# Delta-rule attention and two MoE layers on one core: order of the start, a joint product in step 1, PSUM rings by step, and reordered lists and tokens

## The chip, the cores and the metric

The kernel runs on one core of one Trainium2 chip as one program. The metric is the device time of an execution in microseconds (us). Before the change the median of three executions is 841.74 us (840.85 to 842.69).

## The reference

Inputs: q, k, v of shape (4 batches, 8 heads, 768 positions, 48), beta (4, 8, 768); float64 weights for the first MoE layer, float32 for the second. Three layers follow each other.

```python
# 1 attention, per batch and head, 768 positions in sequence
k_n = k / (norm(k) + 1e-6)
y[t] = q[t] @ state
state = state + beta[t] * outer(k_n[t], v[t] - k_n[t] @ state)
# 2 first MoE, x is y laid out as 3072 tokens x 384
x = ((x @ w1) * (x @ w2)) @ w3 @ w_out          # 384 -> 1024 -> 1024 -> 384
# 3 second MoE, 8 experts, each token goes to one
logits = x @ w_gate + modality_bias[modality_id]
e = argmax(logits); gate = softmax(logits)[e]
out = gate * (relu(x @ e_w1[e]) @ e_w2[e])      # 384 -> 1024 -> 384
```

## The kernel before, in words

**Engines and order.** Each engine runs its instructions in the order in which the program issues them: every call goes through `Engine` (L86), which chains an instruction to the one before it on its engine. All of them therefore carry line 86 in the profile, and groups are told apart by tile names. What sets the order is the code itself: the loop over `f` in `moe1`, the calls of `slot(s, f)`, the generators that are advanced one step at a time, and the table `do` in `startup`.

**Numbers.** A float32 product is made of three passes on a high part (rounded to float32r) and a low part (the rest): high by high, low by high, high by low. So nearly every tensor is split: ScalarE copies the high part, VectorE or GpSimd subtracts it to get the low one.

**The start** (`startup`, L561 on) walks a list `todo` of 36 tiles: 8 of w_out, 16 of w3 and 12 of w1 and w2, all float64 in memory. `tick(n)` issues for tile n+1 the magnitude `mag` and the low word (two ScalarE instructions, `scalar`), for tile n two VectorE operations that join them to a float32 (`vector`), then by `flush` what has come due of earlier tiles, then the next load (`issue`) and the products (`use`). `use` folds w3 and w_out into one matrix `w34` (PSUM tile `pw`) and queues the split of a tile (`w34h`, `w34l`, and for w1 and w2 `w`) as one function that makes the high part on ScalarE and the low part on VectorE. w_out, in float32, lies in tiles `wos`; five of its eight rows lie in the space of `X[1]`, so `X[1]` can be cleared or filled only when the last folded tile's products with them are done. Between the ticks `do` inserts the first steps of the attention: gram matrices, the 31-step triangular inverse on VectorE (`tmp`, `Tt`), step 0.

**Attention** takes the positions in 12 steps of 64; a unit is two steps. In step s `chain_k` multiplies the keys with the state (`X[..., 0:48]`), for s > 1 jointly with the queries that lie beside it (`X[..., 48:112]`) in four PSUM tiles `pkq`, takes R = v - that, and `mask_parts` masks the query part on VectorE: the first two tiles at once, the others when `slot` comes to f = 1. `chain_u` gives `pu`, `chain_y` the output `py`, `chain_s` the new state. Step 1 is done otherwise: keys alone (`pk`), and later the queries (`pq`) in `masked`, masked on VectorE. The loads of the queries of steps 1 and 2 are issued in step 1, f = 0. PSUM tiles come from two rings of two buffers, `ps` and `pc`: of a step's four `pkq` the first two lie in `ps` and the others in `pc`, where `pu` lies too.

**First MoE** (`moe1`): twelve blocks of 256 tokens, eight f each; nine products each for w1 and w2 into `pAB`, their product `a` split into `ch` and `cl`, and two f later the products with `w34` into `px`. `slot(i + 1, f)` puts a piece of attention ahead of each f. The end of a block routes its tokens; `place` ranks them one block later (`pr`; then `hot`, one-hot rows and columns; then `pl`, which is added to `list`).

**Second MoE** (`moe2`): 14 slots of up to 256 tokens of one expert. `back(i)` runs eight f of nine products each into `ph`, its split `hh` and `hl`, and two f later six products into `spy`. `ahead` advances the splitting of later weights (`w1h`, `w1l`, `w2h`, `w2l`) and, at f = 1, 2, 3, the tokens of the next slot: a transpose `spt` of gathered rows `xg`, split into `sxh` and `sxl`. During slots 0 to 2 the generator `late` runs one step per f: the last block's `place`, then `listed`, then the tables of the later slots.

## Time and profile before

| | |
|---|---|
| median of 3 executions | 841.74 us |
| the profiled execution | 841.03 us |
| its span, first to last instruction | 839.3 us |
| TensorE busy | 786.3 us, 94% of the span |
| VectorE busy | 618.8 us, 74% |
| ScalarE busy | 408.9 us, 49% |
| GpSimd busy | 165.6 us, 20% |
| mean granted TensorE clock | 0.968 of full speed |

The profile describes one execution, so sums are made against its 841.03 us; 1.7 us of that lie outside the span. The median of the runs is 0.7 us above it. An engine's idle time counts only where another engine, in the end TensorE, waits for it; the busy share is an average over stages with different limits.

### The profile page before, as it was taken

The numbers are of one execution on the slowest core, as the hardware profiler recorded it, in microseconds if no ns is written. First come the engines' busy times: TensorE is split into PE (matmuls) and PEld (weight loads), VectorE is DVE, ScalarE is ACT, GpSimd is POOL, SyncE is SP. The second block draws the span as 40 slices with busy tenths as digits, with TensorE's granted clock in tenths as the row PEclk, the third lists the DMA queues.
The fourth block names the chain that finished last, engine by engine and source line by source line (L and its number), as shares of the span: only waits on it lengthen the run. The fifth ranks groups of instructions, "written<-read, shape, count | busy, mean of one in ns | idle before, by whom it ended". The sixth has DMA issues, their size and how long they took to land.

```text
span 839.3 us, 23624 instructions
## 1 busy us (share of the span) xinstructions
PE 786.3 (94%) x9583; PEld 730.6 (87%) x9583; DVE 618.8 (74%) x1573; ACT 408.9 (49%) x863; POOL 165.6 (20%) x172
## 2 busy tenths in 40 slices
PE   5797789999999999999999999999899999999994
PEld 5664468999999899989998999999799999999983
DVE  5998889769777976897689864567886778677651
ACT  6467673562546154524543353334455655655541
POOL 3021121100000001000100000013254654645420
PEclk8598899999999999999999999999999999999997
DMA  9952563314121421133021401047457678677610
GB/s 310 280 176 87 151 161 102 75 35 120 54 51 38 116 65 40 40 115 82 23 65 39 102 13 31 27 131 222 151 177 246 215 249 258 227 225 238 220 56 6
DMA packets 71812, 105.34 MB, mean 126 GB/s; under 512 B 33988, under 2 KB 53332, under 8 KB 71696
## 3 DMA queue, kind: packets, MB, share of 16 engines
q1 hardware_dynamic: 64464, 88.35, 34.7%
q0 software_dynamic: 4064, 11.06, 3.9%
q10 hardware_dynamic: 3168, 4.34, 1.5%
q8 instruction: 77, 1.26, 0.6%
q14 instruction: 39, 0.32, 0.1%
HBM read 89.15 MB, written 10.63 MB: 119 GB/s over the span
## 4 chain that ended last, share of the span: by engine, by line
PE 46%; DVE 26%; issue 11%; ACT 7%; POOL 4%; DMA 3%; SPq 1%; POOLq 0%; DVEq 0%; ACTq 0%
PE pAB L86 13%; PE px L86 9%; PE ph L86 7%; PE spy L86 4%; DVE tmp L86 4%; DVE Tt L86 4%; DVE X L86 3%; DVE TT L86 2%; PE pw L86 2%; DVE Ab L86 2%; ACT TT L86 2%; PE pkq L86 2%; PE pg L86 2%; DVE a L86 2%; PE py L86 2%
## 5 line engine op out<-in xcount | busy, mean ns | idle before, releaser
L86 PE MATMUL pAB<-x,w 128*128 128x256 f32 x1728 | 228.8, 286 | 0.0
L86 PEld LDWEIGHTS pAB<-x,w 128*128 128x128 f32 x1728 | 213.9, 191 | 4.4
L86 ACT CAST ch<-a 128x256 fp32r<-128x256 f32 x96 | 39.0, 406 | 116.4 <-DVE a L86 116.4
L86 ACT COPY a<-pAB 128x256 f32<-128x256 f32 x96 | 35.6, 371 | 116.9 <-PE pAB L86 104.3
L86 DVE TENSOR_TENSOR a<-a,pAB 128x256 f32<-128x256 f32 x96 | 40.0, 416 | 65.6 <-ACT a L86 65.3
L86 PE MATMUL ph<-sxh,w1h 128*128 128x256 f32 x288 | 82.5, 286 | 0.5 <-DVE hl L86 0.5
L86 ACT ACTIVATE hh<-ph 128x256 fp32r<-128x256 f32 x96 | 37.0, 385 | 91.7 <-PE ph L86 91.5
L86 PE MATMUL ph<-sxl,w1h 128*128 128x256 f32 x288 | 81.2, 282 | 0.0
L86 PE MATMUL ph<-sxh,w1l 128*128 128x256 f32 x288 | 81.2, 282 | 0.0
L86 DVE SCALAR_TENSOR_TENSOR hl<-ph,hh 128x256 fp32r<-128x256 f32 x96 | 40.3, 420 | 41.0 <-ACT hh L86 40.5
L86 DVE TENSOR_TENSOR Tt<-tmp,Tt 128x31 f32<-128x31 f32 (+15 forms) x186 | 64.3, 346 | 6.4
L86 DVE TENSOR_TENSOR w2l<-r,w2h 128x768 fp32r<-128x768 f32 x56 | 59.5, 1074 | 12.2 <-ACT w2h L86 11.9
L86 DVE TENSOR_TENSOR tmp<-Ab,Tt 128x31 f32<-128x31 f32 (+15 forms) x186 | 65.4, 352 | 3.0
L86 PE MATMUL px<-w34h,ch 128*128 128x392 f32 x192 | 65.6, 342 | 0.0
L86 PE MATMUL px<-w34h,cl 128*128 128x392 f32 x192 | 65.3, 340 | 0.0
L86 PE MATMUL px<-w34l,ch 128*128 128x392 f32 x192 | 65.2, 339 | 0.0
L86 POOL TENSOR_TENSOR w1l<-r,w1h 128x512 fp32r<-128x512 f32 x39 | 51.0, 1327 | 49.9 <-ACT w1h L86 49.6
L86 DVE TENSOR_TENSOR cl<-a,ch 128x256 fp32r<-128x256 f32 x96 | 43.0, 447 | 20.1 <-ACT ch L86 19.3
L86 PEld LDWEIGHTS ph<-sxh,w1h 128*128 128x128 f32 x288 | 54.7, 190 | 1.3 <-DVE hl L86 1.1
L86 PEld LDWEIGHTS ph<-sxh,w1l 128*128 128x128 f32 x288 | 54.8, 190 | 0.0
L86 PEld LDWEIGHTS ph<-sxl,w1h 128*128 128x128 f32 x288 | 54.6, 190 | 0.0
L86 ACT CAST w1h<-r 128x512 fp32r<-128x512 f32 x84 | 49.5, 615 | 2.9 <-DMA r<-in_e_w_dram 2.5
(269 smaller groups left out, 1677.7 us busy)
## 6 DMA issues: line engine op xcount, KB each, us to landing
r<-in_e_w_dram SPq DMA_DIRECT2D x42, 512.0 KB, 4.7
r<-in_e_w_dram SPq DMA_DIRECT2D x56, 384.0 KB, 3.9
raw<-in_w_dram SPq DMA_DIRECT2D x28, 512.0 KB, 4.6
kT<-in_kt_dram SPq DMA_DIRECT2D x12, 512.0 KB, 4.5
X<-in_q_dram SPq DMA_DIRECT2D x24, 256.0 KB, 4.8
vt<-in_v_dram SPq DMA_DIRECT2D x12, 384.0 KB, 4.7
kb<-in_kb_dram SPq DMA_DIRECT2D x12, 384.0 KB, 4.7
x2d<-xr ACTq DMA_DIRECT2D x22, 192.5 KB, 2.8
```

Of the source, the lines that this page charges most:

```text
L86: x = f(*a, **kw)
```

## The change

- **Start.** The split of a tile is queued as two entries, one in `high` (ScalarE) and one in `low` (VectorE). `tick` issues the due high parts ahead of the next tile's magnitude, and the low parts where both were before. `flush`, which the last ticks call first, now issues other work, then high parts, then low parts.
- **Step 1** takes the joint form that the later steps have. Its masks are made by a ScalarE copy and a GpSimd select for each half tile (eight of each) in place of four VectorE products. The queries of steps 1 and 2 are loaded at the last folded tile of the start.
- **Rings by step.** In odd steps the first two `pkq` lie in `pc` and the others in `ps`; in even steps as before.
- **Second MoE.** In slots 0 to 2 `late` issues `pl` one f later (f = 4). In slot 0 the next slot's tokens are issued ahead of the weights of the same f; in slot 2 they come at f = 3, 4, 5.

```diff
         if f == 0:
             self.chain_k(s)
-            if s == 1:
-                self.queries(1)
-                self.queries(2)
         elif f == 1:
             if c == 0:
                 list(self.merge1(u))
                 next(self.work, None)
                 if more:
                     self.work = self.inverse(u + 1)
-            if s > 1:
-                list(self.masks)
+            list(self.masks)
         elif f == 2:
             list(self.chain_u(s) if c else self.merge2(u))
-            if s == 1:
-                list(self.masked(s))
             if s + 1 < NS:
                 self.values(s + 1)
         elif f == 3:
...
+                nc.scalar.copy(W[o:o + C, h, a:a + HP], pq[o:o + C])
+                nc.gpsimd.affine_select(out=W[o:o + C, h, a:a + HP], in_=W[o:o + C, h, a:a + HP], pattern=[[0, HP], [1, C]], compare_op=ALU.is_gt, fill=0.0, base=0, channel_multiplier=-1)
...
-        if s > 1:
...
-                pool, tag = ((self.ps, "ps"), (pc, "pc"))[q // 2]
...
-            self.R = R
-            self.masks = self.mask_parts(s, todo)
-            next(self.masks)
-            return
-        for a in self.halves:
-            pk = pc.tile([P, HP, D], F32, tag="pc", name="pk")
-            for n, m, h in self.tiles(a):
-                o, w = (1 - h) * C, h * C
-                nc.tensor.matmul(pk[o:o + C, m], kT[w:w + C, n0 + n], X[w:w + C, h, n, 0:D], start=True, stop=True)
-            nc.vector.tensor_tensor(out=R[:, a:a + HP], in0=vt[:, a:a + HP], in1=pk, op=ALU.subtract)
+        todo = []
+        for q, a in enumerate(range(0, NP, NQ)):
+            pool, tag = ((self.ps, "ps"), (pc, "pc"))[(q // 2 + s) % 2]
+            pk = pool.tile([P, NQ, D + C], F32, tag=tag, name="pkq")
+            for m in range(NQ):
+                for h in range(2):
+                    o, w = (1 - h) * C, h * C
+                    nc.tensor.matmul(pk[o:o + C, m], kT[w:w + C, n0 + a + m], X[w:w + C, h, a + m], start=True, stop=True)
+            todo.append((a, pk))
+        for a, pk in todo:
+            nc.vector.tensor_tensor(out=R[:, a:a + NQ], in0=vt[:, a:a + NQ], in1=pk[:, :, 0:D], op=ALU.subtract)
         self.R = R
+        self.masks = self.mask_parts(s, todo)
+        next(self.masks)
 
     def mask_parts(self, s, todo):
 
@@ -483,6 +464,10 @@
         for q, (a, pk) in enumerate(todo):
             for h in range(2):
                 o = (1 - h) * C
+                if s == 1:
+                    self.nc.scalar.copy(W[o:o + C, h, a:a + NQ], pk[o:o + C, :, D:])
+                    self.nc.gpsimd.affine_select(out=W[o:o + C, h, a:a + NQ], in_=W[o:o + C, h, a:a + NQ], pattern=[[0, NQ], [1, C]], compare_op=ALU.is_gt, fill=0.0, base=0, channel_multiplier=-1)
+                    continue
                 self.nc.vector.tensor_tensor(out=W[o:o + C, h, a:a + NQ], in0=pk[o:o + C, :, D:], in1=mb[o:o + C], op=ALU.mult)
             if q == 1:
...
+        raw, out, mag, after, high, low = {}, {}, {}, [], [], []
...
-            due = n + 1 if kind == "w" else min(n + 2, FC) if kind == "o" else n + (2 if n < FC + AHEAD else 4)
+            when = min(n + 2, FC) if kind == "o" else n + (2 if n < FC + AHEAD else 4)
...
-                def f():
-                    nc.scalar.copy(self.w34[0][:, r], pw)
-                    nc.vector.tensor_tensor(out=self.w34[1][:, r], in0=pw, in1=self.w34[0][:, r].bitcast(F32), op=ALU.subtract)
+                high.append((when, lambda: nc.scalar.copy(self.w34[0][:, r], pw)))
+                low.append((when, lambda: nc.vector.tensor_tensor(out=self.w34[1][:, r], in0=pw, in1=self.w34[0][:, r].bitcast(F32), op=ALU.subtract)))
+                return
             else:
                 m, g, kk = x
                 t = wp.tile([P, 2, DCH], F32R, tag=f"w{m}{g}{kk}", name=f"w{m + 1}")
                 hi, lo = self.w12[m][0][g][kk], self.w12[m][1][g][kk] = t[:, 0], t[:, 1]
 
-                def f():
-                    nc.scalar.copy(hi, out[n])
-                    nc.vector.tensor_tensor(out=lo, in0=out[n], in1=hi.bitcast(F32), op=ALU.subtract)
-            after.append((due, f))
+                high.append((n + 1, lambda: nc.scalar.copy(hi, out[n])))
+                low.append((n + 1, lambda: nc.vector.tensor_tensor(out=lo, in0=out[n], in1=hi.bitcast(F32), op=ALU.subtract)))
+                return
+            after.append((when, f))
+
+        def due(n, lists):
+            for x in lists:
+                now = [y for y in x if y[0] <= n]
+                x[:] = [y for y in x if y[0] > n]
+                yield from (f for _, f in now)
 
         def flush(n):
-            now = [f for due, f in after if due <= n]
-            after[:] = [x for x in after if x[0] > n]
-            for f in now:
+            for f in due(n, (after, high)):
+                f()
+            for f in due(n, (low,)):
                 f()
 
         def tick(n):
             self.n = n
             if n >= NSTART - 2:
                 flush(n)
+            for f in due(n, (high,)):
+                f()
             scalar(n + 1)
             vector(n)
-            flush(n)
+            for f in due(n, (low, after)):
+                f()
             issue()
             use(n)
...
         folded = todo.index(("3", K3 - 1))
-        do.setdefault(folded, []).append(self.clear)
+        do.setdefault(folded, []).extend([self.clear, lambda: self.queries(1), lambda: self.queries(2)])
         do.setdefault(folded + 1, []).append(lambda: split(self.chain_s(0)))
         do.setdefault(NSTART - 1, []).extend([lambda: self.tokens(1), lambda: self.tokens(2)])
...
         def late():
             yield
-            yield from self.place(NT // MT - 1)
+            last = self.place(NT // MT - 1)
+            next(last)
             yield
+            next(last)
+            yield
+            yield
+            list(last)
             yield from self.listed()
             yield
             yield from self.late_slots()
...
             def step(tok, n):
+                if tok and i == 0:
+                    next(toks, None)
                 for _ in range(n):
                     next(work, None)
-                if tok:
+                if tok and i > 0:
                     next(toks, None)
...
-            ahead(f in (1, 2, 3), 1 + (f < 3 if i == 0 else f > 4))
+            ahead(f - 2 * (i == 2) in (1, 2, 3), 1 + (f < 3 if i == 0 else f > 4))
```

What ScalarE is given in the start, one piece of the difference, from the last gram matrices of unit 0 to the root `r` of unit 1 (TT_94 is the space of the converted tiles, TT_93 unit 0's inverse):

```order
 L86 ACTIVATE An<-pg 32x8x32 x2
 L86 COPY TT_93<-TT_93 32x32x32 x2
-L86 ACTIVATE mag<-raw 128x512
-L86 ACTIVATE TT_94<-raw 128x512
 L86 CAST w34h<-pw 128x392
+L86 ACTIVATE mag<-raw 128x512
+L86 ACTIVATE TT_94<-raw 128x512
 L86 ACTIVATE mag<-raw 128x512
 L86 ACTIVATE TT_94<-raw 128x512
 L86 COPY An<-pe 32x16x32 x4
 L86 ACTIVATE r<-ss 128x32
```

The copy of `w34h` moves ahead of one tile's two conversions; the same happens at each later split of the start.

What SyncE's queue is given around the end of the start (X_91 and X_90 hold the queries of steps 1 and 2, raw the float64 tiles, kb the tokens of steps 1 and 2):

```order
 L86 DMA vt<-in_v_dram 128x768
-L86 DMA raw<-in_w_dram 128x512 x13
-L86 DMA kb<-in_kb_dram 128x768 x2
+L86 DMA raw<-in_w_dram 128x512 x12
 L86 DMA X_91<-in_q_dram 64x16x64 x2
 L86 DMA X_90<-in_q_dram 64x16x64 x2
+L86 DMA raw<-in_w_dram 128x512
+L86 DMA kb<-in_kb_dram 128x768 x2
```

The four query loads move ahead of the last float64 tile and of kb; they stood behind both.

TensorE in slot 0 of the second MoE, before, at the end of f = 3:

```order
L86 MATMUL ph<-sxh,w1l 128x256
L86 MATMUL spt<-ident,xg 128x128 x2
L86 LDWEIGHTS hot
L86 MATMUL pl<-hot 128x192
L86 LDWEIGHTS hot
L86 MATMUL pl<-hot 128x192
L86 MATMUL spy<-w2h,hh 128x384
```

And after the change, at the end of f = 4:

```order
L86 MATMUL ph<-sxh,w1h 128x256
L86 MATMUL ph<-sxl,w1h 128x256
L86 MATMUL ph<-sxh,w1l 128x256
L86 LDWEIGHTS hot
L86 MATMUL pl<-hot 128x192
L86 LDWEIGHTS hot
L86 MATMUL pl<-hot 128x192
L86 MATMUL spy<-w2h,hh 128x384
```

The two `pl` now come behind the next f's nine `ph` products; the transposes `spt` stay at the end of f = 3 and are followed there by f = 1's six `spy` products.

## Rows read from the trace of the kernel before

**Rows 1.** The page, part 1: busy time, share, instructions of each engine.

```profile
PE 786.3 (94%) x9583; PEld 730.6 (87%) x9583; DVE 618.8 (74%) x1573; ACT 408.9 (49%) x863; POOL 165.6 (20%) x172
```

**Rows 2.** Busy time by stage: stage, length, PE, PEld, DVE, ACT, POOL, clock, DMA.

```profile
44.00:116.00 72.00, 58.23 (x688) 36.17 (x688) 63.47 (x131) 49.81 (x90) 12.46 (x26) 0.91 0.42 130
116.00:160.00 44.00, 42.00 (x711) 39.21 (x709) 38.28 (x78) 22.38 (x48) 8.01 (x8) 1.00 0.51 135
160.00:570.00 410.00, 404.68 (x6242) 385.32 (x6238) 306.79 (x927) 176.13 (x377) 21.07 (x18) 1.00 0.23 63
```

**Rows 3.** TensorE's waits: waiter, releaser; total us, times, longest us.

```profile
PE pu L86 <- DVE X L86: 4.1, 4, 1.4
...
PE pl L86 <- DVE hot L86: 2.2, 3, 1.8
...
PE spt L86 <- DMA xg<-x2d,id: 1.6, 1, 1.6
...
PE py L86 <- DVE X L86: 1.6, 3, 1.0
...
PE spt L86 <- DVE sxl L86: 1.2, 1, 1.2
...
PE pkq L86 <- DVE list L86: 1.0, 2, 0.6
```

**Rows 4.** VectorE's waits between 44 and 118 us, same columns.

```profile
DVE w34l L86 <- ACT w34h L86: 4.2, 4, 2.7
DVE w L86 <- ACT w L86: 2.4, 2, 1.8
```

**Rows 5.** Timeline of ScalarE: start us, us, engine, line, operation, idle before.

```profile
64.16 2.11 ACT L86 COPY TT<-TT 32x1024 f32<-32x1024 f32 x2 [0.79 <-DVE TT L86]
...
67.62 0.49 ACT L86 CAST w34h<-pw 128x392 fp32r<-128x392 f32 x1
...
87.19 1.94 ACT L86 COPY X<-pu 64x384 f32<-64x384 f32 x4 [5.86 <-PE pu L86]
...
90.20 0.60 ACT L86 CAST w<-TT 128x512 fp32r<-128x512 f32 x1
```

**Rows 6.** Timeline of TensorE from the last folded tile to step 2.

```profile
118.81 2.12 PE L86 MATMUL pk<-X,kT 64*64 64x48 f32 x64 [0.41 <-ACT X L86]
...
127.31 1.97 PE L86 MATMUL pq<-X,kT 64*64 64x64 f32 x60
...
160.44 2.52 PE L86 MATMUL pkq<-X,kT 64*64 64x112 f32 x48 [0.19 <-ACT An L86]
```

**Rows 7.** Timeline of GpSimd: step 0's selects, and the clearing of X.

```profile
53.88 3.33 POOL L86 TENSOR_SCALAR_AFFINE_SELECT X<-X 64x512 f32<-64x512 f32 x4 [45.24 <-ACT X L86]
...
114.98 2.80 POOL L86 MEMSET X<- 32x1536 f32 x2 [19.40 <-PE pw L86]
```

**Rows 8.** Tile X, 118 to 130 us: landing of the queries' four DMAs.

```profile
DMA to landing us min/median/max: 5.7/7.7/8.0
```

**Rows 9.** Tile X, 149 to 160 us: landing of step 3's queries.

```profile
DMA to landing us min/median/max: 5.6/5.6/5.6
```

**Rows 10.** Busy time and granted clock around two falls; columns as in rows 2.

```profile
76.00:78.60 2.60, 0.03 (x1) 0.00 (x0) 2.39 (x9) 2.58 (x5) 0.00 (x0) 1.00 0.24 93
...
78.60:85.40 6.80, 4.54 (x7) 2.52 (x8) 6.39 (x21) 1.26 (x3) 0.00 (x0) 0.50 0.22 78
...
597.40:600.90 3.50, 3.50 (x16) 3.50 (x15) 1.49 (x4) 0.00 (x0) 0.00 (x0) 0.51 0.54 214
```

**Rows 11.** Timeline of VectorE: equal products beside the selects and alone.

```profile
53.98 0.67 DVE L86 TENSOR_TENSOR tmp<-Ab,Tt 128x112 f32<-128x112 f32 x1
...
82.40 0.27 DVE L86 TENSOR_TENSOR tmp<-Ab,Tt 128x112 f32<-128x112 f32 x1
```

**Rows 12.** Timeline of VectorE, slot 0 of the second MoE: hl of f = 2.

```profile
595.54 0.42 DVE L86 SCALAR_TENSOR_TENSOR hl<-ph,hh 128x256 fp32r<-128x256 f32 x1
```

**Rows 13.** Timeline of TensorE, slot 0: pl at the end of f = 3.

```profile
596.75 0.64 PE L86 MATMUL pl<-hot 128*128 128x192 f16 x2 [1.84 <-DVE hot L86]
```

More of the change, by code (lines that the diff above doesn't have):

```diff
@@ L420, in masked @@
         kT, W, n0 = self.st[s // US]["kT"], self.st["W", s], s % US * NP
-        mb = self.mask.unsqueeze(1).to_broadcast([P, HP, C])
         todo = []
@@ L433, in masked @@
                 o = (1 - h) * C
-                if s < 1:
-                    nc.scalar.copy(W[o:o + C, h, a:a + HP], pq[o:o + C])
-                    nc.gpsimd.affine_select(out=W[o:o + C, h, a:a + HP], in_=W[o:o + C, h, a:a + HP], pattern=[[0, HP], [1, C]], compare_op=ALU.is_gt, fill=0.0, base=0, channel_multiplier=-1)
-                    continue
-                nc.vector.tensor_tensor(out=W[o:o + C, h, a:a + HP], in0=pq[o:o + C], in1=mb[o:o + C], op=ALU.mult)
+                nc.scalar.copy(W[o:o + C, h, a:a + HP], pq[o:o + C])
+                nc.gpsimd.affine_select(out=W[o:o + C, h, a:a + HP], in_=W[o:o + C, h, a:a + HP], pattern=[[0, HP], [1, C]], compare_op=ALU.is_gt, fill=0.0, base=0, channel_multiplier=-1)
     halves = range(0, NP, HP)
@@ L454, in chain_k @@
         R = a1.tile([P, NP, D], F32, tag="R", name="R")
-        if s > 1:
-            todo = []
-            for q, a in enumerate(range(0, NP, NQ)):
-                pool, tag = ((self.ps, "ps"), (pc, "pc"))[q // 2]
-                pk = pool.tile([P, NQ, D + C], F32, tag=tag, name="pkq")
-                for m in range(NQ):
-                    for h in range(2):
-                        o, w = (1 - h) * C, h * C
-                        nc.tensor.matmul(pk[o:o + C, m], kT[w:w + C, n0 + a + m], X[w:w + C, h, a + m], start=True, stop=True)
-                todo.append((a, pk))
-            for a, pk in todo:
-                nc.vector.tensor_tensor(out=R[:, a:a + NQ], in0=vt[:, a:a + NQ], in1=pk[:, :, 0:D], op=ALU.subtract)
-            self.R = R
-            self.masks = self.mask_parts(s, todo)
-            next(self.masks)
-            return
-        for a in self.halves:
-            pk = pc.tile([P, HP, D], F32, tag="pc", name="pk")
-            for n, m, h in self.tiles(a):
-                o, w = (1 - h) * C, h * C
-                nc.tensor.matmul(pk[o:o + C, m], kT[w:w + C, n0 + n], X[w:w + C, h, n, 0:D], start=True, stop=True)
-            nc.vector.tensor_tensor(out=R[:, a:a + HP], in0=vt[:, a:a + HP], in1=pk, op=ALU.subtract)
+        todo = []
[9 more added lines that the diff above has]
+            nc.vector.tensor_tensor(out=R[:, a:a + NQ], in0=vt[:, a:a + NQ], in1=pk[:, :, 0:D], op=ALU.subtract)
         self.R = R
+        self.masks = self.mask_parts(s, todo)
+        next(self.masks)
     def mask_parts(self, s, todo):
@@ L586, in startup @@
         free = [f"w{m}1{kk}" for kk in range(KC) for m in range(2)] + ["x0", "x1", "xr"]
-        raw, out, mag, after = {}, {}, {}, []
+        raw, out, mag, after, high, low = {}, {}, {}, [], [], []
         issued = [0]
```

## The prediction

> **What bounds the kernel now.** I read the page's shares first, then busy time by stage, then TensorE's waits, and only then timelines around the places that change. TensorE is busy 94% of the span [rows 1], so the question is what each stage leaves it idle for. From 44 to 116 us it is not the bound: VectorE is busy 63.47 of 72 us, TensorE 58.23 [rows 2]. From 116 us on TensorE is: it idles 2.0 us of 44 up to 160, and 5.3 us of 410 up to 570 [rows 2]. After that its waits are few and have names [rows 3]. So an edit pays in two ways only: it shortens VectorE's chain ahead of 116 us, or it removes one of TensorE's listed waits behind it.
>
> **Start: high parts sooner.** VectorE stands still 4.2 us in four waits for `w34h`, and 2.4 us in two for `w` [rows 4]. The reader is to see why in ScalarE's queue: the copies of the inverse end at 66.27, the cast of `w34h` begins at 67.62, with one tile's two conversions (1.3 us) between [rows 5]; with `pu` likewise, whose copies end at 89.13 while the cast of `w` begins at 90.20 [rows 5]. Now the cast comes first. Three of the four `w34h` waits are 4.2 - 2.7 = 1.5 us together, and go. In the longest, of 2.7 us, the low part starts some 1.3 us sooner, but VectorE's next work is the join of the very tile whose conversions now stand behind the cast (0.5 us): 0.6 us are left. The 1.8 us at `w` shrinks by 1.1 (90.20 - 89.13), and by a little more because `pu` starts sooner too. That is 1.5 + 0.6 + 1.1 = 3.2, with the last effect 3.5 us. The other wait for `w`, 2.4 - 1.8 = 0.6 us, lies behind the last folded tile, where the cast now even stands behind the state's copies; I count nothing for it, since TensorE waits for something else there (next part). Bounds: 2.0 (only the short waits and the conversions' half) and 6.0 (4.2 + 1.8).
>
> **Step 1: the joint form.** It needs fewer products: `pk` 2.12 us and `pq` 1.97 x 64/60 = 2.10 make 4.22; a joint `pkq` of step 2 takes 2.52 x 64/48 = 3.36 [rows 6]. That is -0.9 us on TensorE. The waits of `py` for the masks on VectorE, 1.6 us [rows 3], go: ScalarE and GpSimd make the masks two f ahead of `py`, and the four VectorE products vanish.
>
> But the joint product now needs the queries, and they cannot come early. X[1] holds rows of w_out until the last folded products, and the clearing of X[1], which waits for the same products, starts at 114.98 [rows 7]. The load is issued then at the soonest. Before, `pk` started at 118.81 and needed no queries [rows 6]. The four loads of 118 to 130 us land 5.7 to 8.0 us after issue [rows 8], two alone 5.6 [rows 9]. Both halves of step 1 are needed at once, so the product starts between 120.6 (114.98 + 5.6) and 123.0 (114.98 + 8.0). I take 121.8: the first pair of four, with one float64 tile in flight and a second issue behind the first. Cost: 121.8 - 118.81 = +3.0 us, bounds +1.8 and +4.2, in a place where everything behind it on TensorE, the first MoE included, queues up. On SyncE the last float64 tile and both kb now stand behind four query loads; they are used several us later, so I count nothing; if that cover is gone it shows as waits of ScalarE's last conversions.
>
> TensorE is idle from 118.40 (118.81 - 0.41) until then, 3.4 us. After 2.6 us without work from 76 us on the granted clock was 0.50 for 6.8 us, and it was 0.51 for 3.5 us after the waits of 1.2 and 1.8 us near 592 and 597 [rows 3, 10]. So I expect a fall to 1.2 GHz here too, of the shorter kind: 3.5 us at half clock cost 1.7 us. Bounds 0 and 3.4.
>
> **GpSimd's selects beside VectorE.** Four selects of 64 x 512 take 3.33 us [rows 7], so eight of half the size about as much. Beside them a product of VectorE took 0.67 us where an equal one alone took 0.27 [rows 11]; the one after it reads the same way, 0.8 us in all. VectorE has lost 2.8 us of masks here, so I count nothing; bounds 0 and 3.3, the selects' whole time. The Trainium skill ("SBUF — State Buffer", section "Who interferes with whom") says that a VectorE operation with two SBUF inputs is blocked for the whole of a GpSimd instruction that reads SBUF. By the rule all 3.3 us would be lost on VectorE; the trace shows a quarter, since most of VectorE's work then was not of that kind or not in step with a select.
>
> **Rings by step.** Four times `pu` waits for masks on VectorE, 4.1 us, the longest 1.4 [rows 3]; all four lie in odd steps, because `pu` needs a buffer of `pc` and the late masks (those of f = 1) still read there. In odd steps the early masks now free `pc`, and the late ones hold `ps`. The two waits of `pkq` for `list`, 1.0 us [rows 3], were for the second `ps` buffer and are passed two products later. What is late next is VectorE's product `a`, which frees the PSUM of the f after next; VectorE is idle a quarter of that stage, 410 - 306.79 us [rows 2]. -5.1 us; bounds -5.1 and -1.0.
>
> **Second MoE.** In slot 0 `spt` waits 1.2 us for `sxl`, and `pl` 1.8 us for `hot` [rows 3]. The first shrinks to about 0.5, as the tokens are now split ahead of one weight part. The second goes, but VectorE frees `ph` of f = 2 only at 595.96 (595.54 + 0.42) [rows 12]; TensorE was done with `spt` at 594.91 (596.75 - 1.84) [rows 13], is there 0.6 sooner, at 594.3, and has six `spy` products ahead of that `ph`. So a new wait of less than 1.7 (595.96 - 594.3) takes the old one's place; I take 0.6. So 3.0 - 0.5 - 0.6 = 1.9 us go, and with them the fall of the clock, 3.5 us at half [rows 10], 1.7 us. -3.6; bounds -1.0 and -4.7. In slot 2 `spt` waits 1.6 us for gathered rows [rows 3]; two f later, with some thirty products between, they should have landed. -1.6; bounds 0 and -1.6. `list` itself is issued one f later, but `listed` follows where it did, so tables and gathers don't move.
>
> **The sum**, against the profiled execution's 841.03 us: -3.5 + 3.0 + 1.7 - 0.9 - 1.6 = -1.3 up to step 2; -5.1 for the rings; -3.6 - 1.6 in the second MoE. That is -11.6, so 829.4. The median of the runs lies 0.7 above that execution: 830.1, predicted as 830.
>
> **Rivals.**
> 1. The start brings nothing. Queries land at 8.0 us (+4.2), the clock falls for 6.8 us as at 78.6 (+3.4), the casts give only 2.0: -2.0 + 4.2 + 3.4 - 0.9 - 1.6 = +3.1. With the other terms (-10.3) 833.8. For it: small loads at 8.0 in rows 8; against: less traffic beside them. 0.15.
> 2. The rings move the wait: VectorE, with equal work, makes TensorE wait one product later, only the 1.0 of `list` stays: 829.4 + 4.1 = 833.5. For it: VectorE 306.79 of 410 us busy; against: a quarter of the stage is idle on it. 0.10.
> 3. The start goes well: all 6.0 us of waits gone, landing at 5.6 (+1.8), no fall: 6.0 - 1.8 + 0.9 + 1.6 = 6.7 gained, 841.03 - 6.7 - 10.3 = 824.0. 0.10.
> 4. Selects block VectorE for their whole 3.3 us, and TensorE waits for its products: 832.7. Rows 11 show 0.8 of 3.3, so 0.04. This is the skill's rule named above.
> 5. Slower: the clock falls at the queries' wait and stays low while VectorE, busy 38.28 of 44 us [rows 2], paces TensorE. At half clock from 123 to 155 us that is 32/2 = 16 in place of 1.7, with 1.2 for the later landing: 829.4 + 14.3 + 1.2 = 844.9. It decides from about 26 us at half clock on, the forecast's 11.6 + 1.7 doubled. For it: in rows 10 a fall outlasted 4.5 us of work; against: TensorE is busy 42.0 of 44 us here, at half clock always, and a fully busy stretch ended the fall at 600.9. 0.05.
>
> **Chances.** Forecast 0.52 (827 to 832.5 by itself), rivals as given, and 0.04 that rivals 1 and 2 meet and slot 0 gives little, which ends within 0.2% (1.7 us, about what a measurement of this kernel tells from no change). Faster 0.91, same 0.04, slower 0.05. The range for 8 in 10 leaves out rival 5, the case of no change and half of rival 3: 825 to 836.5.
>
> **What will show it.** Right: no VectorE waits for `w34h` over 1 us ahead of 110 us; the last folded products 3 to 4 us sooner; `pkq` of step 1 as the first wait of TensorE for a DMA of X, about 3 us, and a clock of 0.5 behind it; no `py` wait in step 1; no `pu` wait in steps 3 to 9; clock 1.00 from 590 us on; no `spt` wait for `xg`. Wrong: a `pAB` or `pu` wait for VectorE in odd steps, a `ph` wait of over 1 us in slot 0, or `pS` not sooner than now.

## The result, and the profile after

The changed kernel takes 830.96 us, the median of four executions (829.33 to 833.54), against 842.22 (840.85 to 842.96) for the kernel before: ratio 0.9871, 95% interval 0.9839 to 0.9903. Run again later beside other kernels it took 829.14 against 839.3: ratio 0.9888, interval 0.9871 to 0.9904. By these ratios, at 840 us, it is 9.4 to 10.8 us faster. The prediction was 11.6 us less than the execution it was summed against, 830 as a median.

The profiled execution is the slowest of the first four, 833.54 us with a span of 831.8. Its shares, against [rows 1] (PE is TensorE, PEld its weight loads, DVE VectorE, ACT ScalarE, POOL GpSimd):

```profile
PE 787.1 (95%) x9519; PEld 730.8 (88%) x9519; DVE 617.7 (74%) x1571; ACT 411.3 (49%) x871; POOL 170.1 (20%) x180
```

The stages of [rows 2] in the same columns (stage, length, PE, PEld, DVE, ACT, POOL, clock, DMA), and one stretch more:

```profile
44.00:116.00 72.00, 61.19 (x732) 37.79 (x733) 64.16 (x132) 49.73 (x90) 14.13 (x27) 0.91 0.45 136
116.00:160.00 44.00, 41.22 (x596) 39.30 (x590) 33.60 (x73) 23.81 (x53) 8.80 (x13) 0.92 0.50 125
160.00:570.00 410.00, 409.26 (x6285) 390.20 (x6285) 310.66 (x942) 180.47 (x386) 26.09 (x23) 1.00 0.24 66
118.90:125.70 6.80, 5.86 (x62) 5.88 (x62) 4.65 (x9) 4.57 (x9) 1.28 (x4) 0.50 1.14 291
```

From 160 to 570 us TensorE now idles 0.7 us where it idled 5.3 [rows 2]. From 116 to 160 it is no better off, and its mean granted clock there is 0.92 instead of 1.00: the whole loss of clock lies in the 6.8 us of the last row. TensorE's waits, against [rows 3]:

```profile
PE pkq L86 <- DMA X<-in_q_dram: 2.8, 2, 1.7
...
PE ph L86 <- DVE hl L86: 1.5, 2, 1.1
...
PE pkq L86 <- ACT An L86: 0.7, 2, 0.4
PE spy L86 <- ACT hh L86: 0.7, 1, 0.7
...
PE spt L86 <- DVE sxl L86: 0.5, 1, 0.5
```

`pu`, `pl`, `py` for masks, `spt` for the gathered rows `xg` and `pkq` for `list` are gone from the list. The waits for the queries and for `hh` are new, and `ph` waits 1.5 us for `hl` where it waited 0.5. VectorE's waits from 44 to 118 us, against [rows 4]:

```profile
DVE w34l L86 <- ACT w34h L86: 1.4, 1, 1.4
DVE w L86 <- ACT w L86: 1.1, 1, 1.1
DVE TT L86 <- ACT TT L86: 0.7, 1, 0.7
DVE x L86 <- ACT x L86: 0.6, 1, 0.6
```

In this window 6.6 us have become 3.8, but that flatters the change: one more wait ends just behind the window.

```profile
118.69 0.69 DVE L86 TENSOR_TENSOR w<-TT,w 128x512 fp32r<-128x512 f32 x1 [4.14 <-ACT w L86]
```

This is the cast behind the state's copies, as long in the second profile below (4.13 us). Up to 112 us, ahead of it, VectorE's waits are 6.0 us before, 3.8 in this profile and 3.7 in the second one. Step 1 on TensorE, against [rows 6]:

```profile
115.04 1.64 PE L86 MATMUL pS<-X,kb 64*48 64x48 f32 x64
118.35 0.37 PE L86 MATMUL pkq<-X,kT 64*64 64x112 f32 x2 [1.67 <-DMA X<-in_q_dram]
119.84 6.11 PE L86 MATMUL pkq<-X,kT 64*64 64x112 f32 x62 [1.11 <-DMA X<-in_q_dram]
125.87 4.57 PE L86 MATMUL pAB<-x,w 128*128 128x256 f32 x36
130.38 2.07 PE L86 MATMUL pu<-R,TT 64*64 64x48 f32 x64
```

`pS` starts 1.7 us sooner than before (116.76), but step 2's `pkq` at 160.70, 1.4 later than before (159.27). A second profiled execution of the same kernel (829 us) reads otherwise in the same view:

```profile
114.16 1.64 PE L86 MATMUL pS<-X,kb 64*48 64x48 f32 x64
117.04 0.37 PE L86 MATMUL pkq<-X,kT 64*64 64x112 f32 x2 [1.24 <-DMA X<-in_q_dram]
118.38 3.25 PE L86 MATMUL pkq<-X,kT 64*64 64x112 f32 x62 [0.97 <-DMA X<-in_q_dram]
121.56 4.57 PE L86 MATMUL pAB<-x,w 128*128 128x256 f32 x36
```

The waits are the same and together 0.6 us shorter. The clock stays at 1.00, the same products take 3.25 instead of 6.11 us, and step 2 starts at 156.64, 2.6 sooner than before. So a fall of the clock in this place costs 2.9 us, and it comes in one execution and not in another. Slot 0 of the second MoE, against [rows 13], in the first profile:

```profile
584.76 0.38 PE L86 MATMUL ph<-sxh,w1h 128*128 128x256 f32 x1 [0.46 <-DVE hl L86]
586.62 0.44 PE L86 MATMUL spt<-ident,xg 128*128 128x128 f32 x2 [0.54 <-DVE sxl L86]
591.51 0.39 PE L86 MATMUL ph<-sxh,w1h 128*128 128x256 f32 x1 [1.08 <-DVE hl L86]
592.68 0.34 PE L86 MATMUL pl<-hot 128*128 128x192 f16 x2
```

`pl` waits for nothing, the clock is 1.00 throughout, and from the first `spt` of the stage (slot 0's own tokens) to the first that slot 1 issues it takes 28.7 us instead of 31.9.

### The profile page after: what moved, and what is told of

Its sections match the earlier page's. It is cut to its first block, busy times and chain, and to the rows that moved or that the text cites. A ratio compares the mean times of both kernels' runs of the same rounds, so it can differ in the third digit from the quotient of the medians.

```text
span 831.8 us, 23509 instructions
## 1 busy us (share of the span) xinstructions
PE 787.1 (95%) x9519; PEld 730.8 (88%) x9519; DVE 617.7 (74%) x1571; ACT 411.3 (49%) x871; POOL 170.1 (20%) x180
## 4 chain that ended last, share of the span: by engine, by line
PE 68%; DVE 11%; issue 9%; POOL 4%; DMA 3%; ACT 2%; SPq 1%; POOLq 0%; ACTq 0%; DVEq 0%
PE pAB L86 24%; PE px L86 16%; PE ph L86 8%; PE pkq L86 5%; DVE TT L86 3%; PE spy L86 3%; PE pu L86 3%; PE py L86 3%; DVE tmp L86 2%; DVE Tt L86 2%; PE pS L86 2%; POOL w1l L86 2%; DMA X<-in_q_dram 2%; PE pg L86 1%; DMA raw<-in_w_out_dram 1%
## 5 line engine op out<-in xcount | busy, mean ns | idle before, releaser
L86 ACT CAST ch<-a 128x256 fp32r<-128x256 f32 x96 | 39.0, 406 | 121.8 <-DVE a L86 121.8
L86 DVE SCALAR_TENSOR_TENSOR hl<-ph,hh 128x256 fp32r<-128x256 f32 x96 | 40.2, 419 | 37.1 <-ACT hh L86 36.7
L86 DVE TENSOR_TENSOR cl<-a,ch 128x256 fp32r<-128x256 f32 x96 | 40.8, 425 | 20.1 <-ACT ch L86 19.3
```

The source lines that it names most:

```text
L86: x = f(*a, **kw)
```

## The experiments

A ratio is to the kernel before in the same group of runs, with its 95% interval; a hundredth of a per cent is 0.084 us. Kernels of different groups are compared by their ratios.

**1. Rings alone.** Edit, on the kernel before:

```diff
-                pool, tag = ((self.ps, "ps"), (pc, "pc"))[q // 2]
+                pool, tag = ((self.ps, "ps"), (pc, "pc"))[(q // 2 + s) % 2]
```

> The kernel before with one part of the change alone: from step 2 on the rings go by step, all else as before. Theory: the rings are the largest part. In the changed kernel's trace the odd steps 3 to 9 became 1.0, 1.7, 1.5 and 1.6 us shorter, and the waits of pkq for list went too, about 6 us from step 2 to the second MoE, so 842.2 - 6.3 = 836 us, and no pu wait for VectorE between 160 and 570 us. Rival (the prediction's size): the four waits and the list's, 5.1 us, so 837. Rival (the wait moves): TensorE waits for VectorE one product later when the rest of the change isn't there, 841 to 842.

Measured: 833.53 against 840.43, ratio 0.9919 (0.9906 to 0.9932), -6.8 us. Of TensorE's waits from 160 to 570 us one is left:

```profile
PE pkq L86 <- ACT An L86: 0.2, 1, 0.2
```

From step 2's `pkq` to the second MoE's first `ph` it takes 421.8 us, before 427.4: 5.6 less. The wait didn't move to another product; the theory holds. Slot 0 took 30.4 instead of 31.9 us, with the waits of before (1.15 us for `sxl`, 1.85 for `hot`) but at a clock of 1.00 throughout:

```profile
592.49 0.64 PE L86 MATMUL pl<-hot 128*128 128x192 f16 x2 [1.85 <-DVE hot L86]
```

```profile
592.40:600.90 8.50, 8.27 (x58) 8.20 (x59) 6.55 (x17) 3.33 (x6) 0.00 (x0) 1.00 0.57 185
```

That isn't the rings' doing: with the old rings slot 0 took 30.4 in the tenth experiment, also without a fall, and 31.9 in the second, with one.

**2. The start alone.** `use`, `due`, `flush` and `tick` as changed, the rest as before.

> The kernel before with one part of the change alone: the start's high parts on ScalarE ahead of the next tile's magnitude, low parts apart; step 1, rings and the second MoE as before. Theory: only about 2 us of the 3.5 predicted come out, since the casts that now stand first on ScalarE wait themselves for VectorE (0.8 and 1.9 us in the changed kernel) and hold up the magnitudes behind them: pS starts 1.7 to 2.2 us sooner, 842.2 - 2 = 840 us. Rival (the prediction's size): -3.5, 838.7. Rival: the gain of the start is eaten before the attention's steps follow, 842.

Measured: 841.5, ratio 1.0011 (0.9999 to 1.0024): nothing, or a loss. Yet `pS` starts at 113.64, 3.1 us sooner. VectorE shows where they go:

```profile
117.29 0.69 DVE L86 TENSOR_TENSOR w<-TT,w 128x512 fp32r<-128x512 f32 x1 [4.13 <-ACT w L86]
...
121.93 1.01 DVE L86 TENSOR_TENSOR R<-vt,pk 128x384 f32<-128x384 f32 x2
```

ScalarE's cast of `w` now stands behind the state's copies, which wait for GpSimd's clearing. VectorE waits 4.1 us for it, with `R` behind. `R` comes 1.5 us sooner than before (123.48), not 3.1, and so do the masks, for which TensorE waits:

```profile
135.35 0.30 PE L86 MATMUL py<-X 128*64 128x64 f32 x2 [2.42 <-DVE X L86]
```

Behind that wait the clock fell for 3.4 us. Step 2 starts 45.2 us after `pS`, before 42.5, and so only 0.45 us sooner than before. The theory (-2) was wrong; the third reading, that the gain is eaten before the steps follow, is right.

**3. The changed kernel with the old step 1.** `chain_k`, `masked`, `mask_parts` and the queries' place as before the change.

> The changed kernel with step 1 as before: keys alone (pk), queries loaded at step 1's first f and multiplied and masked later, masks on VectorE. High parts first, rings by step and the second MoE as changed. Theory: the joint form with the queries it has to wait for costs more than it saves. In the changed kernel's trace step 2 starts 1.4 us later than before although the start's last products came 1.7 us sooner: 3.1 us lost, so this kernel is about 3 us faster than the changed one, 828 us (ratio to before 0.983), with pk starting at 117 us, no wait for a DMA of X, and the clock at 1.00 there. Rival (the prediction's balance): the joint form costs 2.2 net (3.0 + 1.7 - 0.9 - 1.6), 829. Rival: the joint form pays because the masks leave VectorE, and this kernel is slower than the changed one, 832 or more.

Measured: 831.08, ratio 0.9899 (0.9883 to 0.9915). That is 0.9 to 2.4 us slower than the changed kernel by the ratios, with overlapping intervals; it isn't 3 us faster. My theory rested on the one execution with a long fall. `pk` starts at 116.10, no DMA is waited for, but `py` waits 2.4 us for the masks as in the second experiment, here without a fall of the clock. The first line is the wait, the second the stretch behind it in this experiment, the third that stretch in the second experiment (columns as in [rows 2]):

```profile
135.76 0.30 PE L86 MATMUL py<-X 128*64 128x64 f32 x2 [2.40 <-DVE X L86]
```

```profile
136.60:139.80 3.20, 2.91 (x69) 2.71 (x66) 3.13 (x8) 1.30 (x3) 0.00 (x0) 1.00 0.00 0
```

```profile
136.60:139.80 3.20, 3.20 (x51) 2.99 (x47) 3.10 (x9) 1.30 (x3) 0.28 (x1) 0.50 0.00 0
```

**4. The second MoE alone.** `late`, `step` and the line of `ahead` as changed.

> The kernel before with one part of the change alone: in the second MoE pl one f later, tokens ahead of weights in slot 0 and at f = 3, 4, 5 in slot 2. Theory: slot 0 gives 3.1 us (the waits for hot and sxl shrink and the clock doesn't fall), slot 2 nearly nothing (0.1 us), since the later tokens meet the weights' low parts on VectorE and GpSimd and new waits of TensorE take the place of the one for the gathered rows: 842.2 - 3.2 = 839 us. Rival (the prediction's size): 3.6 + 1.6 = 5.2, 837. Rival: slot 0's gain hangs on when the attention ends, and alone it is 1 us or less, 841 to 842.

Measured: 837.78, ratio 0.9966 (0.9954 to 0.9978), -2.9 us. Slot 0 takes 28.8 instead of 31.9 us; from slot 1's first transpose to slot 3's it takes 37.2, before 37.1. The theory holds: in this pair of profiles all of it is slot 0.

**5. The changed kernel again.** No edit.

> The changed kernel itself, once more, beside the kernel before on one chip with the other kernels of this group, and for a second profile of it. If the time of the first comparison holds, the ratio to before is 0.987, 829.6 us where before takes 840.4. Theory: what the first profile shows at step 1 is typical: queries land after the state's copies, the clock falls to a half behind the wait, and step 2 starts 45.7 us after pS (42.5 before, 44.1 with the old step 1). Then this kernel is no faster than the changed kernel with the old step 1, whose ratio was 0.9899 (0.9883 to 0.9915). Rival: the first profile was of an execution with a long fall, others have a shorter one or none, and the joint step 1 is worth 2 us: ratio 0.987, and a profile in which step 2 starts 44 us or less after pS.

Measured: ratio 0.9888; step 2 starts 42.5 us after `pS`, the second profile above. The rival holds for that profile; the ratio lies between both expectations.

**6. Slot 2's tokens at the old place.**

```diff
-            ahead(f - 2 * (i == 2) in (1, 2, 3), 1 + (f < 3 if i == 0 else f > 4))
+            ahead(f in (1, 2, 3), 1 + (f < 3 if i == 0 else f > 4))
```

> The changed kernel with slot 2's tokens back at f = 1, 2, 3. Theory: the later place brings next to nothing, since the wait for gathered rows is replaced by waits for hh and hl and slot 2 took 0.1 us less than before: here the xg wait of 1.6 us is back, the other waits gone, and the time is the changed kernel's within 0.5 us. Rival (the prediction's term): 1.6 us slower than the changed kernel.

Measured: 831.04, ratio 0.9898 (0.9883 to 0.9913), 0.8 us above the changed kernel in the same group, with overlapping intervals: unclear by the times. The `xg` wait is back (1.7 us). By the traces slots 1 and 2 take 37.2 us here, 37.0 and 36.4 in the changed kernel's two profiles: 0.2 to 0.8 us gained, where the fourth experiment shows 0.1 lost.

**7. TensorE's wait filled.** Ahead of step 1's `pkq`:

```diff
+        if s == 1:
+            pf = self.ps.tile([P, HP, D], F32, tag="ps", name="fill")
+            for x in range(96):
+                m, h = x // 2 % HP, x % 2
+                o, w = (1 - h) * C, h * C
+                nc.tensor.matmul(pf[o:o + C, m], kT[w:w + C, n0 + m], kT[w:w + C, n0 + m, 0:D], start=True, stop=True)
```

> The changed kernel with 96 products of the keys with themselves (64 x 48, as long as pk's, 0.033 us each, 3.2 us in all) ahead of step 1's pkq, whose sums nothing reads: they fill TensorE's wait for the queries. Theory: the clock falls in that wait because TensorE stands still, and the fall costs 2.7 us of the 6.1 that pkq took; with the wait filled the clock stays at 1.00, pkq takes 3.4 us, and the kernel is 2 to 3 us faster than the changed one. Rival: the fall costs nothing in the end, because R comes from VectorE only at 123.3 to 124.5 us and pu has to wait for it: within 1 us of the changed kernel, with a pu wait for R. Rival: the filling delays pkq, 1 us slower.

Measured: 834.72, ratio 0.9944 (0.9931 to 0.9958), 4.7 us slower than the changed kernel by ratio, 5.6 by median. I had misread the count: a product of float32 shows as two rows of the profile, so 96 make 192.

```profile
116.18 4.25 PE L86 MATMUL fill<-kT 64*64 64x48 f32 x139
121.24 1.77 PE L86 MATMUL fill<-kT 64*64 64x48 f32 x53 [0.81 <-issue]
122.79 3.30 PE L86 MATMUL pkq<-X,kT 64*64 64x112 f32 x64
```

`pkq` starts 8.1 us after `pS`, its bulk (62 of its 64 rows) in the fifth experiment 4.2: the filling makes it 3.9 us late. As a test of the price it failed, but it tells two things. With TensorE at work the clock stayed at 1.00 in this profile. And TensorE's lateness here counts in full: step 2 starts 46.5 us after `pS` instead of 42.5, and 4.7 to 5.6 us are lost. The reverse, that a shorter wait for the queries gains as much, isn't shown by this, and the eleventh experiment speaks against it.

**8. Queries in pieces.** Pairs 0 to 13 of one half and 2 to 15 of the other one folded tile earlier:

```diff
...
-        do.setdefault(folded, []).extend([self.clear, lambda: self.queries(1), lambda: self.queries(2)])
+        do.setdefault(folded, []).extend([self.clear, lambda: self.queries(1, ((0, NP - 2, NP), (1, 0, 2))), lambda: self.queries(2)])
+        do.setdefault(todo.index(("3", K3 - 2)), []).append(lambda: self.queries(1, ((1, 2, NP), (0, 0, NP - 2))))
```

> The changed kernel with step 1's queries loaded in four pieces: 14 of 16 pairs of each half one folded tile earlier, where the rows of w_out that lie there have been used, and only the remaining two pairs of each half at the last folded tile. Theory: pkq waits for the state's copies alone, as pk did before (2.0 us after the start of pS; in the changed kernel the bulk of pkq starts 4.8 us after it), the clock doesn't fall, and step 1 shrinks by 2.4 us of wait and up to 2.7 of half clock: 3 to 5 us faster than the changed kernel, ratio 0.982. Rival: R is then what comes last, VectorE's queue lets it start at 123 us only, and 1 to 2 us are gained. Rival: the early loads delay the float64 tiles beside them, and nothing is gained.

Measured: 828.76, ratio 0.9872 (0.9857 to 0.9887), 1.3 us below the changed kernel, intervals overlapping. `pkq` starts with the copies, and its second product waits:

```profile
115.25 0.40 PE L86 MATMUL pkq<-X,kT 64*64 64x112 f32 x2 [0.41 <-ACT X L86]
118.10 4.91 PE L86 MATMUL pkq<-X,kT 64*64 64x112 f32 x62 [2.45 <-DMA X<-in_q_dram]
```

It waits for a piece an eighth the size of a half, issued behind 111.7 us, that lands 5.6 us after its issue, as the halves do in the fifth experiment (5.6 in the median). The bulk starts 4.9 us after `pS`, in the changed kernel's profiles 4.8 and 4.2, and the clock fell for 3.4 us. The theory fell by its own condition, that `pkq` waits for the state's copies alone: the late piece holds pairs 0 and 1, which `pkq` needs first. The eleventh experiment puts that right.

**9. The old step 1 with the cast in front.** On the kernel of the third experiment:

```diff
-            for f in due(n, (after, high)):
+            for f in due(n, (high, after)):
```

> The changed kernel with the old step 1 (as the experiment of that name), and in the last ticks of the start the high parts ahead of the state's copies on ScalarE, where they were before the change. Theory: with the old step 1, VectorE is what makes R late: the cast of the last tile waits on ScalarE behind the state's copies, which wait for GpSimd's clearing, and VectorE stood still 4.1 us for it; R came only 1.5 us sooner than before though pk came 2.7 to 3.1 sooner. With the cast back in front R comes about 1.3 us sooner, the wait of py for the masks shrinks from 2.4 to 1.1 us, and the kernel is 1 to 2 us faster than the old step 1 without it (ratio 0.9899): 0.988. Rival: VectorE is late by its sheer work, the cast's place changes nothing: 0.990.

Measured: 829.9, ratio 0.9871 (0.9845 to 0.9896): 2.4 us faster than without, by ratio, with overlapping intervals. VectorE:

```profile
114.90 0.69 DVE L86 TENSOR_TENSOR w<-TT,w 128x512 fp32r<-128x512 f32 x1 [0.68 <-ACT w L86]
119.46 0.69 DVE L86 TENSOR_TENSOR w<-TT,w 128x512 fp32r<-128x512 f32 x1 [1.64 <-ACT w L86]
121.40 1.01 DVE L86 TENSOR_TENSOR R<-vt,pk 128x384 f32<-128x384 f32 x2
```

`R` comes 6.7 us after the start of `pS` (114.70); in the second and third experiments 8.3. `py` waits 1.1 us for the masks instead of 2.4, and step 2 starts 42.5 us after `pS` instead of 44.1, with a clock of 1.00 in both: 1.6 us. By its traces the theory holds. The times don't tell this kernel, which has no joint step 1, from the changed one.

**10. The joint step 1 alone.** On the kernel before, rings as before.

> The kernel before with one part of the change alone: step 1 in the joint form, its masks on ScalarE and GpSimd, queries loaded at the last folded tile. Theory: by itself it brings nothing or loses: 0.9 us of products and 1.6 us of py's waits go, the wait for the queries costs 2.2 us, and in some executions the clock falls behind it, 2.9 us: 840 to 842 where before takes 840, ratio 1.000 to 1.003. Rival (it pays by itself): without a fall of the clock 842.2 - 0.9 - 1.6 + 2.2, ratio 0.9985 or less. The parts alone and their sum: start 1.0011, rings 0.9919, second MoE 0.9966; with this one at 1.000 they make 0.990, the changed kernel had 0.987 to 0.989.

Measured: 842.45, ratio 1.0018 (1.0002 to 1.0034), +1.5 us. The size is as expected, the cause another. The queries cost 2.2 us of wait and no fall here, but:

```profile
132.43 2.11 PE L86 MATMUL pu<-R,TT 64*64 64x48 f32 x64 [3.00 <-ACT X L86]
```

With the old rings step 1's late masks, ScalarE's copies, hold the `pc` buffers for `pu`. TensorE waits 3.0 us, and the clock falls for 3.4 us behind it. The joint step 1 needs the new rings.

**11. Rows of w_out laid out otherwise.** The one row that the last folded tile reads lies under the last four pairs of a half:

```diff
-        big = self.X[1].rearrange("p h n t -> p (h n t)")[:, 0:5 * XW]
+        big = [self.X[1][:, h, n0:n1].rearrange("p n t -> p (n t)")[:, 0:k * XW].rearrange("p (g n) -> p g n", n=XW) for h, n0, n1, k in ((0, 0, 11, 3), (1, NP - 4, NP, 1), (0, NP - 4, NP, 1))]
...
-        do.setdefault(folded, []).extend([self.clear, lambda: self.queries(1), lambda: self.queries(2)])
+        do.setdefault(folded, []).extend([self.clear, lambda: self.queries(1, ((0, NP - 4, NP),)), lambda: self.queries(2)])
+        do.setdefault(todo.index(("3", K3 - 2)), []).append(lambda: self.queries(1, ((1, 0, NP), (0, 0, NP - 4))))
```

> The changed kernel with the rows of w_out laid out otherwise in X[1]: the one row that the last folded tile still needs lies under the last four pairs of one half, the four others elsewhere in X[1], so seven eighths of step 1's queries are loaded one folded tile earlier, and the last piece is needed only by the last quarter of pkq. (With pairs 0 and 1 in the late piece pkq's second product had to wait until 4.9 us after pS.) Theory: pkq starts 2.0 us after pS and ends 5.7 us after it (7.4 in the changed kernel without a fall of the clock, 10.8 with one); TensorE isn't idle long enough for a fall, and the kernel is 2 to 4 us faster than the changed one, ratio 0.985. Rival: R on VectorE is last then, or the fall comes behind the last quarter's wait: within 1 us of the changed kernel, 0.988.

Measured: 828.05, ratio 0.9848 (0.9824 to 0.9872).

```profile
114.41 1.64 PE L86 MATMUL pS<-X,kb 64*48 64x48 f32 x64
116.46 3.58 PE L86 MATMUL pkq<-X,kT 64*64 64x112 f32 x64 [0.41 <-ACT X L86]
124.47 2.07 PE L86 MATMUL pu<-R,TT 64*64 64x48 f32 x64
```

There is no wait for a DMA and no fall, and `pkq` ends 5.6 us after `pS`, as worked out. But step 2 starts 42.5 us after `pS`, as in the changed kernel without a fall, because `pAB` now waits 1.8 us for VectorE's `a`:

```profile
131.19 2.42 PE L86 MATMUL pAB<-x,w 128*128 128x256 f32 x18 [1.23 <-DVE a L86]
```

So without the wait for the queries VectorE comes last, and nothing is gained over the execution without a fall. This profile and the next have no fall; that none comes in any execution isn't shown.

**12. Both.** The kernel of the eleventh with the cast in front.

> The kernel with the moved rows of w_out, and the high parts of the start's last ticks ahead of the state's copies as well. Theory: in the joint form R doesn't wait for VectorE's queue (it waits for pkq), so the cast's place brings nothing here: the same as with the moved rows alone, within 0.5 us. Rival: with pkq ending sooner VectorE's queue is what comes last, and the cast in front is worth 1 us or more.

Measured: 827.8, ratio 0.9844 (0.9819 to 0.9869). The times don't tell it from the eleventh. That doesn't make the cast's place worth nothing, for the two profiles differ in a second way: here `pkq` waited 1.8 us for the queries, which in the eleventh had landed in time. Even so the wait for `a` is gone, and step 2 starts 41.8 us after `pS`, 0.7 sooner than there. By ratio these two are 2 to 4 us faster than the changed kernel, and the best of all; as they didn't run in one group with it and the intervals touch, that they beat it is likely and not certain.

## Why the prediction was right

The total holds (-11.6 predicted, -9.4 to -10.8 measured), in part by luck. Each part alone, by its ratio at 840 us: rings -6.8 (predicted -5.1), second MoE -2.9 (-5.2). By these ratios the rings gave more than predicted and the second MoE less, and the misses cancel for the most part. What the changed kernel has beyond these two, start and step 1 together, is 0.9888 against 0.9919 + 0.9966 - 1 = 0.9885, so nothing; by its first ratio -1.2 (predicted -1.3). The intervals of these ratios are each 1 us wide or more to either side, so they can't tell nothing from -1.3.

The stages of all the profiles together tell it better, for the same start or slot comes out differently from one execution to the next by as much as some terms are worth. In us, from a named first instruction to another:

| stage | old form | new form | mean difference | predicted |
|---|---|---|---|---|
| to `pS` | 116.2 to 118.1 (4 profiles) | 113.2 to 115.0 (10) | -2.9 | -3.5 |
| `pS` to step 2's `pkq` | 42.5 (3, old start and step 1) | 45.7, 42.5, 45.5 (first, fifth, sixth) | +2.0 | +2.2 |
| step 2's `pkq` to the first `ph` | 425.9 to 427.4 (4) | 421.0 to 421.8 (10) | -5.4 | -5.1 |
| slot 0 | 31.9, 31.9 with a fall, 30.4, 30.4 without (4) | 28.7 to 28.8 (10) | -2.4 | -3.6 |
| slots 1 and 2 | 37.1 to 37.6 (5) | 36.4 to 37.2 (9) | -0.4 | -1.6 |

Their sum is -9.1, 2.5 less than predicted. The start, step 1 and the rings are close to the prediction; nearly all that it had too large lies in the second MoE.

- **Start, -3.5.** The three short waits for `w34h` went in the first profile (in the second one of 1.0 us is left), and the longest shrank from 2.7 to 1.4, by the 1.3 reckoned. The sign "no wait for `w34h` over 1 us" so failed, but it didn't fit the prediction's own working. `pS` came 1.7 us sooner than in the one profile before in the first profile, 2.6 in the second, 3.1 in the second experiment; the table gives 2.9 in the mean. VectorE's new wait of 0.7 us, at 67.45, is for the conversions behind the cast of that longest wait, and the prediction had reckoned with it. What I missed: a cast ahead on ScalarE can itself wait for VectorE's join (0.8 and 1.9 us at 92.8 and 99.1) and hold up what stands behind it, and behind the second of these stands the other new wait, 0.6 us for `x`.
- **The cast behind the state's copies, 0.** VectorE waits 4.1 us there. In the changed kernel TensorE doesn't wait for what is late by it, so the reason given was right for this kernel. In the second profile `R` stands behind VectorE's queue, not behind `pkq`, and is done at 123.6, well ahead of `pu` at 126.06:

```profile
122.45 1.14 DVE L86 TENSOR_TENSOR R<-vt,pkq 128x192 f32<-128x192 f32 x4
```

Where the wait for the queries is gone it begins to count: TensorE waits 1.8 us for `a` in the eleventh experiment, and no longer in the twelfth. With the old step 1 it costs 1.6 us by the traces (third against ninth), 2.4 by the ratios, and together with the fall behind the wait for the masks it is why the start alone brings nothing.
- **Wait for the queries, +3.0.** `pk` started 2.05 us after `pS`, the bulk of `pkq` 4.8 and 4.2 us after it: +2.8 and +2.2. Its length was right, even if the clock time of 121.8 was late, as `pS` moved too. That all of it is paid for is not shown: in the eleventh experiment the wait is gone and step 2 starts no sooner after `pS`.
- **Clock, +1.7.** 2.9 or 0: two of the three profiles with this start and step 1 have the fall (first and sixth), one has not (fifth). The mean is about right, but that is luck: the fall comes or stays away from one execution to the next, and where it came it lasted 6.8 us and not the 3.5 predicted. It makes 2.9 of the 4.5 us between the two profiled executions of the changed kernel; for the other executions it isn't shown.
- **Products -0.9, masks -1.6, selects 0.** 62 of the 64 rows of `pkq` took 3.25 us where the clock stayed up, as reckoned (3.36 for 64, instead of 4.22), and no `py` waits for masks. Beside the selects at 133 us VectorE's products `tmp` and `Tt` took 0.51 us, else 0.42; three such, 0.3 us:

```profile
133.05 0.43 DVE L86 TENSOR_TENSOR Tt<-tmp,Tt 128x255 f32<-128x255 f32 x1
133.51 0.51 DVE L86 TENSOR_TENSOR tmp<-Ab,Tt 128x256 f32<-128x256 f32 x1
...
135.28 0.51 DVE L86 TENSOR_TENSOR Tt<-tmp,Tt 128x255 f32<-128x255 f32 x1
```

```profile
133.07 2.44 POOL L86 TENSOR_SCALAR_AFFINE_SELECT X<-X 64x256 f32<-64x256 f32 x4 [7.02 <-ACT X L86]
```

The selects stretched too, to 0.48 to 0.68 us each from 0.41 for the four at 124 us, and took 4.3 us in all instead of the 3.3 reckoned. Rival 4 isn't borne out. The Trainium skill ("SBUF — State Buffer", section "Who interferes with whom") has a VectorE operation with two SBUF inputs contend with a GpSimd instruction that reads SBUF for ports that are an exclusive lock. By that rule up to the selects' 2.44 us would have been lost on VectorE, an estimate; the trace disagrees for this kind of GpSimd instruction.
- **Rings, -5.1.** Right in mechanism and nearly in size: 5.6 us in the trace of the first experiment, 5.4 in the table. The 1.5 us that slot 0 is shorter in the first experiment's profile come from the clock, which stays up there in the tenth experiment's profile too, with the old rings. Why the times of the first experiment show 6.8 and not 5.6 stays open. Rival 2 (the wait moves) has fallen.
- **Slot 0, -3.6.** 3.2 us in the first profile, 3.1 in the fourth experiment, but against a profile before in which the clock fell. The prediction counted that fall (1.7) as always there; in two of the four profiles with the old second MoE it is absent, and against those 1.6 us are gained. The new `ph` wait is 1.1 instead of 0.6, and the sign "a `ph` wait over 1 us" stood for a failure that it only half was.
- **Slot 2, -1.6.** This is the step that failed: between 0.1 us lost and 0.8 gained in single profiles, 0.4 gained in the mean. The `xg` wait went, and waits for `hh` and `hl` (0.9 us in the first profile, 0.5 in the second) took its place. In the first profile a token's `sxl` stands behind a weight's low part on VectorE (last section); that this sharing is the whole cause is argued, not shown. The prediction asked only whether the rows had landed, not what the split would meet.

Rival 1 (the start brings nothing) describes the executions with the fall: in the first profile step 2 starts 1.4 us later than before, in the second 2.6 sooner. Its loss of 3.1 us wasn't reached there. Rivals 3 and 5 didn't come.

## What to carry to other kernels

Ask of a buffer ring (buffers used in turn) which reader holds it when the next writer comes, in every step: one line of tile placement was worth more than the rest of this change. When instructions move ahead in one engine's queue, list what each of them may itself wait for, and who then stands behind it. Parts of a change measured alone don't add up where one part makes room for another: start and joint step 1 each gained nothing alone, and the joint step needed the rings. And read a stage in several executions before its length goes into a sum: a fall of the clock that is there in one profile may be absent from the next.

## What the runs showed of the hardware

The clock's fall behind a wait isn't decided by the wait's length alone. After TensorE's wait of 2.4 us for step 1's masks the granted clock was 0.50 (the lower of its two levels, 1.2 of 2.4 GHz) for 3.4 us in the second experiment, and stayed 1.00 in the third, with the same instructions ahead of it. After slot 0's waits of 1.15 and 1.85 us it fell for some 3.5 us in the kernel before and in the second experiment, and stayed 1.00 in the first and the tenth. Behind the waits for the queries it was 0.50 for 6.8 us after 2.8 us of waiting (first profile) and after 2.5 (sixth experiment, 1.4 of it put down to the state's copies), for 3.4 us after 2.9 (eighth), and stayed 1.00 after 2.2 (fifth, tenth) and 1.8 (twelfth); these rows alone would also fit a rule by length.

In slot 2 of the first profile a low part on VectorE, 0.95 us as a rule, took 3.75 beside two GpSimd products of 2.56 us together:

```profile
629.18 3.75 DVE L86 TENSOR_TENSOR w2l<-r,w2h 128x768 fp32r<-128x768 f32 x1 [0.30 <-ACT w2h L86]
632.85 0.41 DVE L86 TENSOR_TENSOR sxl<-spt,sxh 128x256 fp32r<-128x256 f32 x1
...
635.91 0.94 DVE L86 TENSOR_TENSOR w2l<-r,w2h 128x768 fp32r<-128x768 f32 x1
```

```profile
629.54 2.56 POOL L86 TENSOR_TENSOR w1l<-r,w1h 128x512 fp32r<-128x512 f32 x2
```

It lost 2.8 us, about all of GpSimd's time, and the tokens' `sxl` waited behind it. The selects cost a tenth of that. The rule of the Trainium skill named above ("SBUF — State Buffer", section "Who interferes with whom") fits this pair of instructions in that one of the two stood still, and not the selects. By the rows VectorE's product stood still although it had started 0.36 us ahead of GpSimd's; why it was that one stays open.
